# Packed diagonal attention blocks, transposed feature maps and fixed copy engines in a two-layer attention kernel

## The chip, the cores and the metric

One core of a Trainium2 chip runs the whole program. The time is device microseconds of one execution; the median of three runs of the kernel before is 514.66 us (514.08 to 518.85). The engines are named as in the profile: PE (TensorE matmul), PEld (its weight load), DVE (VectorE), ACT (ScalarE), POOL (GpSimd), SP (SyncE, which issues most transfers).

## What is computed

Two pairs of layers, A then B, each with a residual, on x of 1 x 2048 x 512 in bf16, 32 heads of 16 features:

```python
def _A_ref(x, wq, wk, wv, wo, beta):          # 4 segments of 512 tokens
    ...
    phi = lambda t: jnp.where(t > 0, t + 1.0, jnp.exp(t))
    for s in range(N):
        ...
        p = _softmax(logits + causal mask inside the segment)   # logits = q k^T / 4
        a_dot = p @ vs
        a_mem = (phi(qs) @ M) / (phi(qs) @ z + 1e-06)
        o = g * a_mem + (1.0 - g) * a_dot
        M, z = M + phi(ks)^T vs, z + sum(phi(ks))
    return o @ wo
def _B_ref(x, wqkv, w_phi, wo):               # linear attention over all tokens
    pq, pk = q @ w_phi, k @ w_phi
    phi_q = concat(softmax(pq), softmax(-pq)); phi_k likewise
    return ((phi_q @ (phi_k^T v)) / (phi_q @ sum(phi_k) + 1e-06)) @ wo
x = x + A(layernorm(x)); x = x + B(layernorm(x)); and both once more
```

## The kernel before

All of x stays in SBUF (`X`, 16 tiles of 128 tokens). A segment is four tiles. Scores are computed with the keys on the partitions, so that one exponential yields the weights of the product with the values, and a 17th column of the values gives the softmax's sum.

**Attention of a segment** (`a_att`, L1152) runs over pairs of query tiles, (0,1) and (2,3); in the last segment over (0,1), (2) and (3), `LAST` at L1392. Head features are 16 wide; keys are kept twice, with the odd or the even heads set to zero (`KT`, `KTo`), so that 32 rows of PE serve one head. A strip is one PSUM pair of banks of 128 x 1024: matmuls of 32 rows, two or one query tiles wide. Each strip gets one exponential on ACT (L1199) into a `PT` buffer (12 of them, L850), and its diagonal blocks are masked by POOL with `affine_select` (L1203). Two strips on different row groups are issued side by side (`rows`, `mate`). After the strips of a group of eight heads come the products with the values (17 columns each), a reciprocal (L1222) and a scaling for each tile (L1224), then the addition of the memory part `AM` (L1233), a transpose, the output projection and the residual (`a_out` L1243, `residual` L1239).

**Projections** (`a_proj`, L1057): at the first segment of each layer (`by_pe`) keys are projected feature-major for the scores (16 matmuls of 128 columns a tile) and once more token-major (4 matmuls of 512 columns, L1085) for phi (L1025: an exponential on ACT, a minimum and a maximum-plus-sum on DVE), which the memory state needs (`a_state`, L1108).

**Layer B**: `b_keys` (L1251) projects keys and values of a segment, takes both exponentials on ACT (L1261), sums and reciprocals on DVE (L1262, L1264), scales on POOL (L1266; DVE for the last two tiles), and adds into `KV32`; after the last segment `Rkv` (L1295) is formed. `b_queries` (L1300) makes the query features (`EQ`), `b_out` (L1337) the output. B's output of layer 0 runs beside A of layer 1; the last one is the tail, which stores the result.

**Order.** The kernel is written as a list of operations with reads, writes and a cost. `schedule` (L352) lays them on the engines in one pass of a list scheduler: of the operations that could start, the one with the least number in `PLAN` (L44, one number for each operation, in the order in which they are written down) goes first. An operation with two possible engines (`copy`, L784: ACT or DVE) takes the one where it can start earlier. `finalize` (L609) turns the dependencies into semaphore waits, so on the chip the order on each engine is fixed and the times are not. Where PE would be idle too long, idle matmuls are put in (L1448) to keep its clock up.

Of the kernel before, what the change touches and what calls it, by code (L numbers as in the profile page):

```python
# [15 lines left out]
H = 32  # L16
DH = 16
# [9 lines left out]
ENGS = ("pe", "act", "dve", "pool", "sp")  # L27
HOP = dict(pe=0.03, act=0.03, dve=0.03, pool=0.05, sp=0.04)
# [11 lines left out]
OVERLAP = 0.14  # L40
PRI = dict(mem=-5.0, state=0.5, aout=-0.2, lnx0=-0.5, lnx1=-10.0, ap0=9.5, aps=4.625, bo0=-6.0, bo1=3.5, lnb=-7.5, bk=2.0, bks=2.2, kv=14.0, q00=58.0,
# [3 lines left out]
    3, 4, 5, 7, 6, 0, 64, 10, 8, 9, 11, 14, 79, 15, 18, 13, 23, 29, 75, 32, 53, 21, 80, 26, 150, 35, 58, 85, 16, 126, 36, 156, 71, 60, 61, 122, 44,  # L45
    42, 285, 292, 20, 141, 151, 140, 194, 106, 100, 117, 57, 22, 12, 87, 81, 40, 2, 49, 17, 84, 82, 120, 47, 31, 48, 43, 1, 131, 113, 174, 19, 91,
    123, 52, 25, 59, 83, 41, 199, 28, 219, 65, 189, 191, 27, 62, 70, 45, 108, 97, 93, 39, 143, 181, 206, 88, 107, 105, 116, 56, 132, 133, 112, 24,
    154, 142, 127, 95, 157, 54, 37, 76, 186, 144, 51, 172, 188, 200, 134, 148, 192, 165, 135, 236, 218, 177, 149, 74, 248, 257, 266, 158, 69, 169,
    175, 287, 256, 114, 249, 291, 195, 119, 211, 164, 153, 136, 130, 99, 288, 180, 171, 230, 293, 261, 204, 265, 124, 197, 33, 63, 89, 182, 78, 50,
    159, 170, 227, 255, 121, 128, 138, 215, 110, 226, 213, 46, 187, 240, 98, 216, 55, 282, 260, 250, 273, 72, 320, 299, 269, 160, 176, 90, 198, 178,  # L50
    173, 212, 220, 238, 279, 244, 297, 329, 243, 317, 179, 335, 332, 252, 167, 246, 309, 294, 290, 286, 270, 348, 308, 306, 229, 253, 234, 366, 333,
    237, 67, 307, 389, 455, 399, 356, 233, 319, 208, 259, 328, 232, 231, 221, 271, 314, 339, 315, 362, 429, 318, 276, 324, 254, 380, 251, 205, 313,
    344, 360, 417, 454, 377, 342, 338, 353, 334, 387, 347, 382, 402, 416, 446, 376, 331, 401, 323, 361, 495, 396, 383, 235, 438, 436, 365, 464, 394,
    463, 349, 431, 459, 469, 392, 168, 435, 407, 444, 472, 450, 404, 476, 458, 405, 483, 453, 466, 451, 245, 397, 403, 447, 517, 635, 521, 530, 500,
    509, 406, 364, 263, 262, 300, 374, 224, 375, 486, 359, 482, 534, 478, 499, 582, 528, 491, 492, 529, 434, 553, 595, 511, 669, 525, 583, 596, 572,
    533, 38, 66, 145, 102, 155, 161, 77, 147, 185, 30, 125, 96, 103, 163, 111, 109, 92, 73, 321, 311, 296, 203, 386, 330, 340, 423, 357, 388, 275,
    351, 400, 202, 410, 384, 258, 484, 452, 391, 352, 363, 395, 385, 368, 418, 432, 201, 370, 425, 424, 341, 515, 422, 398, 354, 409, 420, 503, 477,
    414, 516, 488, 591, 543, 536, 547, 379, 373, 326, 346, 371, 481, 277, 412, 310, 440, 419, 426, 514, 618, 301, 558, 441, 494, 498, 538, 549, 546,
    465, 487, 457, 433, 523, 214, 34, 68, 101, 184, 118, 217, 129, 86, 193, 302, 268, 225, 152, 312, 139, 350, 267, 280, 274, 281, 272, 305, 284, 322,
    415, 146, 358, 283, 372, 408, 166, 456, 367, 442, 627, 639, 674, 449, 550, 545, 518, 602, 575, 666, 462, 390, 461, 437, 421, 210, 540, 467, 413,  # L60
    460, 470, 445, 617, 493, 513, 471, 604, 489, 519, 508, 662, 657, 631, 510, 640, 764, 625, 660, 679, 655, 690, 664, 701, 724, 837, 758, 846, 673,
    696, 719, 769, 795, 771, 838, 733, 824, 1351, 1380, 1496, 1373, 1318, 1407, 1302, 1304, 1126, 1231, 1201, 1209, 1505, 1467, 1360, 1563, 1434,
    1500, 1595, 1462, 1424, 1567, 1532, 1576, 1425, 1757, 1733, 1596, 1646, 615, 672, 532, 654, 697, 652, 680, 698, 714, 703, 678, 427, 570, 577, 650,
    734, 369, 381, 295, 552, 496, 574, 555, 621, 597, 554, 475, 548, 448, 663, 541, 506, 593, 522, 505, 520, 524, 468, 637, 560, 563, 677, 624, 638,
    587, 692, 526, 649, 694, 798, 581, 571, 504, 544, 535, 598, 556, 630, 613, 497, 539, 629, 573, 584, 607, 603, 623, 659, 706, 502, 501, 485, 578,
    592, 566, 542, 537, 608, 559, 616, 576, 611, 619, 562, 646, 695, 626, 738, 737, 818, 754, 588, 620, 601, 606, 605, 653, 568, 658, 569, 599, 645,
    636, 622, 633, 614, 585, 586, 490, 667, 740, 751, 676, 642, 807, 704, 793, 800, 836, 687, 675, 716, 799, 634, 651, 641, 632, 561, 691, 686, 565,
    689, 699, 700, 710, 661, 763, 743, 708, 439, 813, 829, 759, 746, 723, 791, 775, 861, 713, 839, 756, 712, 776, 762, 773, 788, 770, 801, 772, 711,
    786, 720, 768, 564, 811, 750, 778, 779, 855, 888, 806, 808, 822, 827, 814, 732, 685, 753, 845, 820, 939, 889, 804, 789, 902, 830, 643, 828, 883,
    872, 908, 869, 927, 886, 958, 875, 862, 856, 914, 916, 957, 895, 945, 936, 241, 183, 190, 264, 228, 239, 343, 336, 327, 411, 137, 196, 104, 162,  # L70
    209, 94, 303, 304, 337, 430, 600, 612, 551, 567, 527, 647, 671, 531, 590, 925, 966, 926, 1007, 985, 730, 823, 802, 670, 644, 721, 693, 656, 681,
    628, 665, 705, 843, 702, 707, 783, 728, 832, 792, 648, 731, 715, 742, 755, 739, 774, 825, 682, 870, 803, 741, 780, 819, 726, 579, 849, 787, 557,
    428, 507, 810, 752, 580, 748, 844, 831, 729, 782, 897, 834, 900, 747, 725, 867, 871, 479, 594, 345, 727, 684, 709, 760, 745, 805, 683, 797, 833,
    781, 668, 766, 877, 1064, 962, 784, 717, 1018, 1000, 688, 809, 876, 812, 874, 899, 898, 906, 777, 722, 857, 840, 835, 826, 790, 969, 912, 920,
    842, 858, 903, 994, 901, 963, 1066, 954, 1129, 1096, 1014, 1009, 1164, 1021, 1005, 761, 1161, 1057, 1025, 1039, 1030, 1035, 1040, 1109, 940, 1136,
    989, 1144, 1045, 1029, 817, 1031, 1042, 937, 1026, 1043, 1061, 1083, 1151, 1008, 1038, 1046, 1015, 1149, 896, 1134, 1121, 1063, 1036, 1127, 1217,
    1269, 1493, 1510, 1084, 1171, 1170, 1143, 1049, 1206, 996, 1053, 1123, 1069, 1059, 1140, 1065, 1106, 1067, 841, 735, 854, 880, 971, 1041, 1101,
    1011, 1003, 961, 864, 1060, 955, 1047, 1062, 981, 1087, 1050, 1102, 952, 1022, 1110, 1157, 1128, 1056, 1158, 1006, 1048, 1027, 953, 976, 959,
    1079, 1113, 1028, 1054, 1111, 998, 1017, 1037, 1119, 951, 1090, 1154, 1001, 1104, 1077, 1051, 1116, 1071, 1118, 1159, 1112, 1058, 1117, 1240,
    1241, 1088, 1080, 1160, 1108, 982, 1130, 1082, 997, 1098, 1172, 1074, 1162, 1076, 1175, 1153, 1147, 1232, 1230, 1024, 1182, 1242, 1250, 1207,  # L80
    1270, 885, 821, 848, 744, 892, 894, 922, 923, 873, 610, 609, 907, 933, 918, 850, 749, 868, 863, 757, 950, 924, 932, 860, 930, 1010, 796, 765, 851,
    893, 960, 816, 917, 991, 852, 965, 905, 949, 935, 904, 964, 934, 944, 815, 891, 974, 878, 980, 986, 1002, 859, 1055, 947, 1033, 1004, 968, 847,
    853, 909, 1019, 1034, 972, 882, 992, 1013, 785, 794, 983, 987, 984, 973, 943, 967, 1044, 1023, 1091, 1032, 1142, 1103, 956, 884, 866, 938, 1068,
    1125, 1244, 1204, 1132, 1146, 1156, 1163, 1150, 1233, 1152, 1180, 1073, 1093, 1433, 1094, 1358, 1099, 1178, 1252, 1095, 1374, 1200, 1181, 1251,
    1189, 1248, 1139, 1328, 1215, 325, 393, 298, 316, 278, 355, 474, 443, 589, 473, 242, 115, 223, 289, 222, 247, 512, 480, 378, 207, 921, 929, 910,
    887, 736, 970, 928, 915, 879, 913, 919, 1190, 993, 1020, 718, 865, 881, 911, 942, 890, 946, 1078, 1115, 1089, 1052, 1107, 1085, 990, 767, 948,
    999, 978, 1092, 988, 1097, 979, 1105, 1070, 1075, 1184, 1208, 1277, 1016, 977, 975, 1174, 1081, 1120, 1218, 1249, 1166, 1265, 1273, 1196, 1221,
    1247, 1100, 941, 931, 995, 1234, 1188, 1316, 1122, 1303, 1352, 1193, 1253, 1263, 1375, 1131, 1306, 1259, 1239, 1195, 1312, 1495, 1411, 1410, 1283,
# [91 lines left out]
    3424, 3397, 3445, 3300, 3431, 3443, 3417, 3451, 3435, 3407, 3404, 3439, 3442, 3378, 3296, 3295, 3420, 3398, 3415, 3369, 3367, 3448, 3426, 3441,  # L180
    3352, 3358,
)


class Res:

# [1309 lines left out]
```

## Time and profile before

| | |
|---|---|
| median of three runs | 514.66 us |
| the profiled execution | 518.92 us |
| its span, first to last instruction | 517.3 us |
| PE clock granted, mean | 0.987 |
| idle matmuls (L1450) | 125, 19.7 us |
| exponentials of scores (L1199) | 320, all between 17.5 and 463.7 us |
| products with the values (17 columns) | 2560 |
| row statistics (L1007), DVE | 64 of 683 ns |
| residuals (L1241), DVE | 54 of 682 ns |
| sums of key features (L1262), DVE | 32 of 1212 ns |
| key feature exponentials (L1261), ACT | 64 of 611 ns |

A busy time is the union of an engine's instructions; the mean of a group is of one instruction, from start to modelled end, so that pipelined matmuls add up to more than their busy time. In the last line of each group stands the idle time of the engine just before it and what ended it.

### The profile page before, as it was taken

The numbers are of one execution on the slowest core, as the hardware profiler recorded it, in microseconds if no ns is written. First come the engines' busy times: TensorE is split into PE (matmuls) and PEld (weight loads), VectorE is DVE, ScalarE is ACT, GpSimd is POOL, SyncE is SP. The second block draws the span as 40 slices with busy tenths as digits, with TensorE's granted clock in tenths as the row PEclk, the third lists the DMA queues.
The fourth block names the chain that finished last, engine by engine and source line by source line (L and its number), as shares of the span: only waits on it lengthen the run. The fifth ranks groups of instructions, "written<-read, shape, count | busy, mean of one in ns | idle before, by whom it ended". The sixth has DMA issues, their size and how long they took to land.

```text
span 517.3 us, 16946 instructions
## 1 busy us (share of the span) xinstructions
PE 487.7 (94%) x7194; PEld 306.4 (59%) x7286; DVE 432.3 (84%) x1025; ACT 440.3 (85%) x593; POOL 269.8 (52%) x396
## 2 busy tenths in 40 slices
PE   9989999999999999999999999999999999999997
PEld 6656455656456656656665555655555555565664
DVE  6998789968669888899968788988998677887995
ACT  3989999989999999854599999899999999974443
POOL 5464486635567766230147468456854476631234
PEclk9989999989999999999999999999999999997999
DMA  8956433332200411200115425224433121110034
GB/s 240 272 93 94 79 67 53 38 57 46 49 13 15 59 39 22 26 4 5 22 22 74 55 39 94 54 41 64 63 63 63 23 55 33 13 37 4 4 82 142
DMA packets 94538, 29.96 MB, mean 58 GB/s; under 512 B 86272, under 2 KB 94464, under 8 KB 94464
## 3 DMA queue, kind: packets, MB, share of 16 engines
q1 hardware_dynamic: 93216, 27.83, 30.0%
q10 hardware_dynamic: 1248, 1.06, 0.8%
q8 instruction: 57, 0.93, 0.8%
q14 instruction: 17, 0.14, 0.1%
HBM read 6.32 MB, written 2.10 MB: 16 GB/s over the span
## 4 chain that ended last, share of the span: by engine, by line
PE 52%; ACT 32%; DVE 11%; DMA 2%; issue 2%
PE PS L729 48%; ACT PT L1199 25%; PE PS L1450 3%; DMA xnT<-xn 2%; ACT Ek L1261 2%; ACT phi L1027 2%; DVE stats L1007 1%; PE PS L807 1%; DVE X L1241 1%; DVE O L1358 1%; DVE KV L1293 1%; DVE EQ L1332 1%; DVE Rkv L1295 1%; DVE rd L1357 0%; DVE PhiK L1029 0%
## 5 line engine op out<-in xcount | busy, mean ns | idle before, releaser
L1199 ACT ACTIVATE PT<-PS 128x1024 bf16<-128x1024 f32 x320 | 308.2, 1054 | 10.0 <-PE PS L729 9.1
L1203 POOL TENSOR_SCALAR_AFFINE_SELECT PT<-PT 128x512 bf16<-128x512 bf16 (+2 forms) x280 | 169.7, 617 | 131.7 <-ACT PT L1199 128.0
L729 PEld LDWEIGHTS PS<-VT,PT 128*128 128x128 bf16 x2560 | 78.1, 96 | 23.3 <-issue 5.8
L729 PE MATMUL PS<-VT,PT 128*128 128x17 bf16 x2560 | 85.7, 171 | 0.1
L729 PE MATMUL PS<-QT,KT 32*128 32x256 bf16 (+1 forms) x864 | 77.4, 245 | 4.5 <-ACT PT L1199 2.9
L1266 POOL TENSOR_TENSOR Ek<-Ek,rZ 128x1024 bf16<-128x1024 bf16 x28 | 55.3, 1977 | 44.7 <-DVE rZ L1264 44.7
L729 PE MATMUL PS<-QT,KTo 32*128 32x128 bf16 (+1 forms) x864 | 76.1, 243 | 2.4 <-ACT PT L1199 1.0
L729 PEld LDWEIGHTS PS<-QT,KT 32*128 32x128 bf16 x864 | 32.4, 92 | 39.2 <-ACT PT L1199 24.0
L1261 ACT ACTIVATE Ek<-PS 128x512 bf16<-128x512 f32 x64 | 35.8, 611 | 13.1 <-PE PS L729 12.8
L729 PEld LDWEIGHTS PS<-QT,KTo 32*128 32x128 bf16 x864 | 35.0, 93 | 19.6 <-ACT PT L1199 11.6
L1241 DVE TENSOR_TENSOR X<-X,PS 128x512 bf16<-128x512 bf16 x54 | 36.8, 682 | 11.3 <-PE PS L729 10.7
L1262 DVE TENSOR_REDUCE Zk<-Ek 128x64 f32<-128x1024 bf16 x32 | 38.6, 1212 | 8.2 <-ACT Ek L1261 7.9
L1007 DVE BATCH_NORM_STATS2 stats<-X 128x6 f32<-128x512 bf16 x64 | 43.3, 683 | 1.5 <-DMA X<-in_A_x_dram 0.8
L1013 POOL TENSOR_TENSOR rstd<-rstd,negh 128x2 f32<-128x2 f32 (+1 forms) x38 | 26.3, 694 | 33.3 <-DVE rstd L1011 32.1
L729 PE MATMUL PS<-xnT,WA_q 128*128 128x128 bf16 x512 | 35.9, 221 | 0.1
L729 PE MATMUL PS<-WA_v,xnT 128*128 128x512 bf16 x110 | 31.9, 380 | 2.4 <-issue 1.0
L729 PE MATMUL PS<-WA_k,xnT 128*128 128x512 bf16 x111 | 31.4, 380 | 2.8 <-issue 1.0
L729 PEld LDWEIGHTS PS<-xnT,WA_q 128*128 128x128 bf16 x512 | 29.6, 99 | 7.0 <-issue 2.8
L1224 DVE TENSOR_TENSOR O<-PS,r 128x128 bf16<-128x128 f32 x128 | 31.5, 281 | 1.2
L729 PE MATMUL PS<-WA_o,OT 128*128 128x512 bf16 x115 | 30.0, 380 | 1.4 <-issue 0.6
L729 PE MATMUL PS<-WB_o,OT 128*128 128x512 bf16 x118 | 29.6, 380 | 1.4 <-DVE QT L785 0.5
L1017 DVE TENSOR_SCALAR xn<-X,mv,rstd 128x512 bf16<-128x512 bf16 x64 | 26.9, 430 | 2.0 <-DMA xnT<-xn 0.9
(135 smaller groups left out, 839.1 us busy)
## 6 DMA issues: line engine op xcount, KB each, us to landing
out_dram<-X SPq DMA_DIRECT2D x16, 128.0 KB, 1.8
X<-in_A_x_dram SPq DMA_DIRECT2D x3, 512.0 KB, 10.0
EQ<-in_B_wqkv_dram SPq DMA_DIRECT2D x2, 512.0 KB, 10.5
OT<-O SPq DMA_TRANSPOSE x46, 2.5
xnT<-xn SPq DMA_TRANSPOSE x36, 2.5
WA_o<-in_A_wo_dram SPq DMA_DIRECT2D x1, 512.0 KB, 10.1
WB_v<-in_B_wqkv_dram SPq DMA_DIRECT2D x1, 512.0 KB, 12.3
WB_o<-in_B_wo_dram SPq DMA_DIRECT2D x1, 512.0 KB, 9.9
```

The lines of the kernel that those rows point to most:

```text
L729: return e.matmul(o, l, r, start=st, stop=sp, tile_position=(basep(l), basep(o)))
L1007: self.dve(lambda e, t=t: e.bn_stats(self.stats[:, t, :], self.X[:, t, :]), 0.60, [R("X", t)], [R("stats", t)])
L1013: self.pool(lambda e, ve=ve, n=n: e.tensor_tensor(ve, ve, self.negh[:, 0:1].to_broadcast([128, n]), ALU.pow), 0.76, [R("rstd", t0 + i) for ...
L1017: self.dve(lambda e, t=t, xn=xn: e.tensor_scalar(xn.ap[:], self.X[:, t, :], self.mv[:, t, 0:1], self.rstd[:, t:t + 1], op0=ALU.subtract, o ...
L1199: self.act(lambda e, st=st, pt=pt: e.activation(pt.ap[:].rearrange("p b c -> p (b c)"), self.ps[:, st.slot[0] * 512:st.slot[0] * 512 + 102 ...
L1203: self.pool(lambda e, dv=dv, nd=nd: e.affine_select(dv(), dv(), [[0, 2], [0, nd], [1, 128]] if nd > 1 else [[0, 2], [1, 128]], ALU.is_ge, 0.0,
L1224: self.dve(lambda e, r1=r1, view=view, c=c, g=g: e.tensor_tensor(o[c].ap[:, g, :].rearrange("p (h d) -> p h d", d=DH), view()[:, c, :, 0:1 ...
L1241: self.dve(lambda e: e.tensor_tensor(X[:, t, :], X[:, t, :], self.bank(gen), ALU.add), 0.61, [R("X", t), gen()], [R("X", t)])
L1261: self.act(lambda e, sgn=sgn, Ek=Ek, gen=gen: e.activation(Ek.ap[:, sgn, :], self.bank(gen), ACT.Exp, scale=1.0 - 2.0 * sgn), 512, [gen()] ...
L1262: self.dve(lambda e, Ek=Ek, Zk=Zk: e.tensor_reduce(Zk.ap[:], Ek.ap[:].rearrange("p s (h j) -> p s h j", h=H), AX.X, ALU.add), 1.15, [Ek(0) ...
L1266: scale = lambda e, Ek=Ek, rZ=rZ: e.tensor_tensor(Ek.ap[:].rearrange("p s (h j) -> p (s h) j", j=DH), Ek.ap[:].rearrange("p s (h j) -> p ( ...
L1450: ins = e.matmul(self.ps[:, b * 512:b * 512 + 256], self.warm[:, 0:128], self.warm[:], start=True, stop=True)
```

## The change

1. **Diagonal blocks packed.** In the odd tiles of each pair the two halves of 64 tokens are exchanged in `X` (loads and stores are split accordingly). The scores of the first halves of both tiles' diagonals, for all four groups of heads, go into one extra pair of strips (`ta`, one for each `y`): matmuls of 32 rows, 64 keys and 64 queries, first tile on partitions 0 to 63 and second on 64 to 127. The rest of the two diagonal tiles goes into one strip per group and `y`, whose exponential writes the middle of a wider buffer (`DT`, 4 buffers of 2 x 2 x 384). POOL masks three blocks of 64 queries, one of them copied from `ta`; DVE makes the fourth as the minimum of `ta` and a constant `late`, which is 0 or 3e38. `PT` has 7 buffers, `O` has 2, and `O2` holds both tiles of a pair. The last segment runs in pairs too.
2. **Per pair**: one reciprocal and one scaling for both tiles, one addition of `AM` of 128 x 1024.
3. **Phi of the first keys**: where keys are projected feature-major and phi is wanted, it is taken from that projection and transposed by DMA; the token-major projection falls away there.
4. **Residual by PE**: in the last segment's `a_out`, and in B's output of the first chunk at the layer change, X is added by a matmul with the identity, followed by a copy on ACT or DVE.
5. **Engines**: `ON` lists 63 operations for ACT, 74 for DVE and 3 (`Rkv`) for POOL; `PLAN` is a new list of 3539 numbers (3455 before). Key scaling on POOL is two halves of 128 x 512.
6. Smaller: `vtone` set by one copy per buffer; the helpers `PAIR`, `second` and `xa` are there and switched off.

```diff
+PAIR = 0.0
...
+        for e, some in ON.items():
+            for i in some:
+                ops[i].eng = (e,)
...
-        self.p_PT = slots("PT", 12, [128, 2, 512], BF16)
+        self.p_PT = slots("PT", 7, [128, 2, 512], BF16)
+        self.p_DT = slots("DT", 4, [128, 2, 2, 384], BF16)
...
+            flat = s <= 2 and tt in by_pe
+            if flat:
+                fm = lambda a: a[:].rearrange("p (g c) -> p g c", g=NG)
+                self.phi(t2, lambda t2=t2: fm(t2.ap), lambda gen=gen: self.bank(gen).rearrange("p (g c) -> p g c", g=NG), gen, t2(), shape=fm)
+                self.transposed(lambda tt=tt: seg["PhiK"].ap[:, tt, :].rearrange("p (a c) -> p a c", a=4), lambda t2=t2: t2.ap[:], [t2()], [seg["PhiK"](tt)], False, pre=[seg["PhiK"]])
...
+        i0, i1 = ts
+        full = [[(0, j), (1, j)] for j in range(i0)]
...
+        ta = [self.p_PT.tile() for _ in range(2)]
+        for y in range(2):
+            st = strips(y, ta[y], lambda st, y=y: [x for g in range(NG) for par in range(2) for h in range(2) for b in range(2) for x in [
+                mm(st, b, (2 * g + par) * 64, K2[par], 2 * y + b, g, ts[h] * 128 + 64 * h, 64, 192 * h, 64, p=64 * h)]], kr)
...
+            for y in range(2):
+                dt = self.p_DT.tile()
+                st = strips(y, dt, lambda st, y=y, g=g: [x for par in range(2) for b in range(2) for x in [
+                    mm(st, b, par * 256, K2[par], 2 * y + b, g, i0 * 128, 128, 64, 192)]] + [x for par in range(2) for b in range(2) for x in [
+                    mm(st, b, par * 256 + 192, K2[par], 2 * y + b, g, i1 * 128, 128, 128, 64)]], kr)
...
+                select(0, 0, src=early)
+                P.add(("dve",), lambda e, early=early, block=block: e.tensor_tensor(block(320), early(), self.late[:, None, None, :].to_broadcast([128, 2, 2, 64]), ALU.min),
+                      {"dve": 0.2}, [ta[y](), R("late")], [dt(("x", 320))], lat=0.09, port=True)
+                select(64, 64)
+                select(256, 0, 64)
...
+            mms.append((lambda: (self.bank(gen), self.ident[:], self.X[:, t, :], False, True), 512))
...
-        PAIRS, LAST = ((0, 1), (2, 3)), ((0, 1), (2,), (3,))
+        PAIRS, LAST = ((0, 1), (2, 3)), (((0, 1), (2, 3)))
```

## The prediction

> **What bounds the kernel now.** I read the page's busy times first, then five windows cut at the first and last exponential (L1199) of each layer: start, attention of layer 0, switch, attention of layer 1, tail.
>
> ```profile
> PE 487.7 (94%) x7194; PEld 306.4 (59%) x7286; DVE 432.3 (84%) x1025; ACT 440.3 (85%) x593; POOL 269.8 (52%) x396
> ```
> ```profile
> 0.00:17.50 17.50, 16.21 (x149) 12.01 (x152) 12.53 (x50) 7.49 (x13) 7.12 (x19) 1.00 0.89 269
> 17.50:215.70 198.20, 186.22 (x3008) 116.32 (x3046) 165.92 (x384) 190.66 (x244) 119.74 (x179) 0.98 0.37 58
> 215.70:262.70 47.00, 45.51 (x531) 30.26 (x535) 42.52 (x98) 26.10 (x49) 6.68 (x7) 1.00 0.06 12
> 262.70:463.70 201.00, 191.69 (x3070) 117.86 (x3107) 169.24 (x401) 192.98 (x249) 120.81 (x179) 1.00 0.31 50
> 463.70:517.30 53.60, 48.09 (x447) 29.95 (x452) 42.06 (x94) 23.04 (x43) 15.50 (x12) 0.94 0.21 57
> ```
>
> Columns: length, then busy time of PE, PEld, DVE, ACT, POOL. In the two attention windows (399.2 us) ACT is busy 383.6 us (96%), DVE 335.2 (84%), POOL 240.6 (60%). PE's 95% there overstates it, as the waits and the timeline show:
>
> ```profile
> PEld PS L729 <- ACT PT L1199: 39.4, 101, 1.1
> ...
> ACT PT L1199 <- PE PS L729: 9.1, 19, 1.1
> ```
> ```profile
> 209.50 0.75 PE L729 MATMUL PS<-VT,PT 128*128 128x17 bf16 x24
> ...
> 267.05 0.23 PE L729 MATMUL PS<-QT,KT 32*128 32x128 bf16 x4
> 267.11 0.22 PE L729 MATMUL PS<-QT,KTo 32*128 32x128 bf16 x4
> 267.17 0.28 PE L729 MATMUL PS<-QT,KT 32*128 32x256 bf16 x4
> ```
>
> PE waits for exponentials 39.4 us, the exponentials for PE only 9.1. A 17-column matmul is booked 171 ns (its group's mean), yet 24 of them take 0.75 us, 31 ns each. So ACT bounds attention. Switch and tail run at half of ACT's pace: DVE is busy 90% of the switch, and the chain of waits runs there through DVE and then PE's projections.
>
> **Packed diagonals, ACT.** Today a segment has 40 exponentials of 128x1024, a quarter of each diagonal block (early queries, late keys) being wholly masked. Now the early-half corners of both tiles share one strip: pair (0,1) takes 2+4x2=10, pair (2,3) 2+4x6=26. 36 x 8 segments = 288, not 320. The output of the diagonal ones is strided; no row shows that, the 1006 to 1220 ns spread of L1199 bounds it, and I keep its mean:
>
> ```profile
> L1199 ACT ACTIVATE PT<-PS 128x1024 bf16<-128x1024 f32 x320 | 308.2, 1054 | 10.0 <-PE PS L729 9.1
> ...
> L1203 POOL TENSOR_SCALAR_AFFINE_SELECT PT<-PT 128x256 bf16<-128x256 bf16 x80 | 33.1, 419 | 10.1 <-ACT PT L1199 7.8
> ...
> L1233 DVE TENSOR_TENSOR O<-O,AM 128x512 bf16<-128x512 bf16 x24 | 12.3, 524 | 0.2
> ```
>
> 32 x 1.054 = 33.7 us less on ACT, all in attention: 349.9 left.
>
> **DVE.** Added: 128 minima with the constant `late`, 128x256. Nearest is L1233, 524 ns at twice the size, 0.27 by proportion; ends 0.20 (its least is 373, halved) and 0.52 (no gain from the smaller size). 128 x 0.27 = 34.6 (26 to 67). Removed: 128 products of 281 ns become 64 of twice the size; with 0.68 us at four times the size (L1358) the line through both gives 0.41, so 36.0-26.5 = 9.5. Reciprocals 72 to 64: about 1. The 24 additions of 524 ns become 12 of about 0.75: 3.6. Attention's DVE: 335.2+34.6-14.1 = 355.7 us.
>
> A rule weighs against this. The Trainium skill, "SBUF — State Buffer", section Who interferes with whom, says that a DVE instruction with two SBUF inputs and a GpSimd instruction reading SBUF exclude each other for a whole instruction. Were every minimum to wait out one 0.419 us select, DVE would have 53.6 us more. The trace agrees in kind (L1233 goes from 373 to 1470 ns, median 424), but its mean already holds such waits. None of the other numbers uses this sentence.
>
> **POOL.** 280 selects (110.4+33.1+28.2 = 171.7 us busy) become 8 segments x 2 pairs x 4 groups x 2 x 3 = 384 at 0.41 = 157. Ek's 28 products of 1.98 us become 56 halves; each pays the fixed part again (about 0.2), 5 us. POOL stays near 58%: nothing. But two selects (0.8 us) follow each diagonal exponential, and the product with values waits for them and the minimum. Behind it on PE stand the next strips, and ACT behind those. Cover: exponentials of the next group, while a PT buffer is free (second rival).
>
> **PE.** 32 strips less, 16 pairs of some 0.25 us: -4. New strips: 64 matmuls of 64 columns per pair of strips. Four 128-column ones start every 60 ns (15 ns each), the 17-column ones every 31; so 64 cost 0.5 (half of 15 ns) to 2.0 us. I take 1.0, the score row being nearest: 16 us. Eight plus four residuals go in by an identity matmul at about 0.22: +2.6. Keys' second projection at each layer's start falls: 32 matmuls at 0.215 = -6.9. Net about +8, covered by PE's 39.4 us of waiting for ACT.
>
> The rule against it: the Trainium skill, "TensorEngine Tiling (Array Packing)", sections Instruction Overhead and Gotcha 2, gives each matmul some 60 cycles however short and denies column tiles the fast weight load. By it the new strips sit at the upper end. No run here shows column tiles. It only weighs on the third rival's chance.
>
> **Plan and copies.** 140 operations get a fixed engine (63 ACT, 74 DVE, 3 POOL). Attention's ACT and DVE together hold 349.9+355.7 = 705.6 us, 353 each if the plan levels them. Today's joint share is 718.8/399.2 = 180 of 200%. With that share 392 us; with ACT's 96% on both, 367. DVE reaches 90% in the switch beside a busy PE, so I take both at 92.5%: 381, -18 us.
>
> **Start** (17.5 us): of the removed projection some 11 matmuls lie before the first exponential, 2.4 us on PE; loads hide part (DMA share 0.89): -1.5, ends 0 and -2.4. The odd tiles' half loads add two issues near 0.5 us on SP's queue ahead of weights: +0.5 (0 to 1). Four phi transposes of about 1.27 us each join SP's full queue (weights' transposes, 19.6 to 30 us); the tiles they delay are used first at 62 us (Ek), so nothing; without that cover 5 us.
>
> **Switch** (47 us): PE chain 242 to 262.7: -3.45 (16 matmuls) +0.9 = -2.6. DVE: six residuals of 0.68 become copies that ACT (26 of 47 us busy) can take, -4.1. But tiles 2 and 3 of segment 3 now end together: statistics, rows, key sums, reciprocal and scaling of tile 2 (0.68+0.17+0.43+1.21+0.54+1.20 = 4.2) move behind the last exponential. Its key exponentials started 5.7 us before tile 3's (223.5 and 229.2), so +2 (0 to 4). Net -0.6. The 4 phi transposes meet an idle queue (DMA share 0.06).
>
> **Tail**: the same delay, +2, less one Rkv product on POOL beside DVE: +1.5. Store halves: 8 more issues, the last one +0.5.
>
> Edits that move nothing: the row normalisation is already DVE's alone (L1017, all 64); the set-up of `late` (3 small POOL operations) and 8 copies merged to 2; `PAIR` is 0, so the new rules of the scheduler stay off; the tail's POOL list names the same tiles.
>
> **Sum**: -18 -1 -0.6 +2 = -17.6 us of the profiled 517.3 us span (518.92 us execution). The median of three is 514.66, so 514.66 x (1-17.6/517.3) = 497.
>
> **Rivals.**
> 1. *ACT alone counted* (DVE fits beside it). 349.9/0.96 = 364, -35, in all -35: 480. For: DVE's waits are mostly on PE and ACT. Against: DVE would have to run at 98%. 12%.
> 2. *PT buffers stop ACT; slower.* PT falls from 12 to 7, two held all pair long by the shared corners; five serve groups needing four. With 36 exponentials in some 48 us, a group of six lasts 8 us; a buffer may be held 5x8/4 = 10 us. I count strip and queue 1.5, rest of its group 4 to 6, selects 0.8 to 1.2, values 56x31 ns = 1.7: 8 to 10.4. Past 10, each us more costs ACT 0.8 a group, in 32 groups 26 us. From 0.7 us beyond, the 18 us are gone; at 1.3 beyond, +33, in all +16: 530. For: no spare at the upper end. Against: diagonal strips can be put first, so that selects lie under the other four. 12%.
> 3. *DVE or PE becomes the bound.* Strips of 2 us on PE (+16) use up its waits and the joint share stays 180%: 392, in all -7. Or minima take 0.52: 32 us more on DVE, at 92.5% (705.6+32)/1.85 = 399, in all 0. So 508 to 515. For: DVE gets the added work and no spare engine takes minima. Against: both prices are ends. 18%.
> 4. *The change does not do what it says*: strips saved but the plan's copies pile on one engine, ACT still 96% at 370: 385, as the forecast; no number of its own, within its chance.
>
> **Chances.** Forecast 58% (own range 487 to 507), rivals 12, 12, 18. One per cent is 5.1 us, about what a measurement of this kernel can tell from no change: 509.5 to 519.8. Faster: 58+12+8 (the part of the third below 509.5) = 78%; within: 10%; slower: 12%, the second rival. Range 480 to 514: it leaves out the second rival and half of the first.
>
> **What would show it.** Right: L1199's successors 288 times, near 1.05 us; ACT in attention 350 to 365 us, DVE 345 to 360, attention windows near 190 us each; switch near 46. Wrong: ACT idle before exponentials for PE strips that wait for values or selects (buffers); minima well over 0.3 us; attention windows near 200 us with DVE over 95%; the corner strips near 2 us on PE.

## The result and the profile after

| | before | after |
|---|---|---|
| median of the runs taken with it | 515.82 us (514.08 to 518.85) | 538.32 us (533.05 to 538.51) |
| ratio | | 1.0405, 95% interval 1.0322 to 1.0488 |
| the profiled execution, its span | 518.92, 517.3 us | 538.30, 536.6 us |
| granted clock, mean of the span | 0.987 | 0.941 |
| clock loss, (1 - clock) x span, mean of runs | 3.9 us | 26.8 us |

The kernel became some 21 us slower by the ratio, 22.5 by the medians, where 18 us faster was forecast. Medians below are over all runs of a kernel; the ratios leave out runs that lay over 1.5% above its fastest. The busy times of the page of after:

```profile
PE 516.5 (96%) x8165; PEld 333.5 (62%) x8165; DVE 444.0 (83%) x1038; ACT 424.3 (79%) x581; POOL 265.4 (49%) x532
```

ACT lost 16 us; DVE gained 12 and PE 29. Of PE's 29 us, 8 are idle matmuls: 192 of 28.0 us where before had 125 of 19.7, with 51 more in the longer start and 24 more in the tail. The five windows of after, cut at its own exponentials as those of before were (columns: length, then PE, PEld, DVE, ACT, POOL, clock, DMA share, GB/s):

```profile
0.00:23.40 23.40, 21.41 (x222) 17.37 (x223) 14.02 (x46) 7.53 (x13) 7.63 (x22) 1.00 0.99 232
23.40:224.70 201.30, 193.90 (x3405) 124.94 (x3405) 167.44 (x390) 180.92 (x237) 116.76 (x242) 0.92 0.37 57
224.70:265.40 40.70, 40.65 (x477) 26.03 (x477) 37.80 (x84) 24.99 (x47) 7.99 (x10) 1.00 0.05 10
265.40:477.50 212.10, 208.12 (x3525) 131.35 (x3525) 178.40 (x425) 184.25 (x240) 116.23 (x242) 0.93 0.31 50
477.50:536.60 59.10, 52.38 (x552) 33.77 (x552) 46.33 (x96) 26.59 (x50) 16.74 (x17) 0.99 0.24 54
```

Against before, the start is 5.9 us longer, attention 3.1 and 11.1, the tail 5.5; only the switch is shorter, by 6.3. In attention PE is busy 97% at a clock of 0.92 to 0.93, ACT 88%. The waits turned round: ACT's exponentials waited 9.1 us for PE before, and 32.6 (19.0 + 9.5, and 4.1 for those of the corners) now:

```profile
ACT DT L1307 <- PE PS L804: 19.0, 28, 2.0
...
PEld PS L804 <- ACT PT L1297: 12.8, 33, 0.8
...
ACT PT L1297 <- PE PS L804: 9.5, 14, 1.8
...
PEld PS L804 <- ACT DT L1307: 8.3, 20, 0.8
```

The costliest groups of the page, for what was added:

```profile
L1313 POOL TENSOR_SCALAR_AFFINE_SELECT DT<-DT 64x256 bf16<-64x256 bf16 (+1 forms) x256 | 107.6, 439 | 88.6 <-ACT DT L1307 87.8
L1307 ACT ACTIVATE DT<-PS 128x1024 bf16<-128x1024 f32 x128 | 130.9, 1040 | 19.5 <-PE PS L804 19.0
L1297 ACT ACTIVATE PT<-PS 128x1024 bf16<-128x1024 f32 x128 | 128.3, 1039 | 10.5 <-PE PS L804 9.5
...
L1313 POOL TENSOR_SCALAR_AFFINE_SELECT DT<-PT 128x256 bf16<-128x256 bf16 x128 | 56.5, 448 | 65.4 <-PE PS L804 47.8
...
L1317 DVE TENSOR_TENSOR DT<-PT,late 128x256 bf16<-128x256 bf16 x128 | 43.9, 351 | 4.5 <-PE PS L804 3.9
```

With the 32 of the corners (L1286, 1031 ns) the exponentials are the 288 forecast, and the strided ones (L1307) cost what the others do. Nothing here is dear enough for 20 us. The granted clock in 40 slices is what stands out, first before, then after:

```profile
PEclk9989999989999999999999999999999999997999
```
```profile
PEclk9965989999999999999999999999999956799999
```

Half clock was granted at 29.8 to 53.7, 429.2 to 449.6 and 453.1 to 463.3 us and in two short spells, 61 us in all; before, 13.6 us. And one place in PE's timeline of after, where a corner strip (tiles 32*64) is issued side by side with a strip of 128-wide tiles:

```profile
426.52 0.22 PE L804 MATMUL PS<-QT,KT 32*64 32x64 bf16 x4
...
426.73 0.53 PE L804 MATMUL PS<-QT,KT 32*64 32x64 bf16 x6
427.19 0.40 PE L804 MATMUL PS<-QT,KTo 32*128 32x192 bf16 x4
427.52 0.20 PE L804 MATMUL PS<-QT,KT 32*128 32x64 bf16 x2
427.65 0.35 PE L804 MATMUL PS<-QT,KTo 32*64 32x64 bf16 x4
```

Four corner matmuls start every 31 to 50 ns until 426.73; from there on the two strips alternate by twos, and the last 16 matmuls take about 1.2 us (the view merges neighbours, so its counts mix the two strips). At full clock such a pair lasts 1.41 us until the next work starts, a corner strip by itself 0.38, a strip of 8 by itself 0.33. There are 13 such pairs: 10 with a strip of 8, 3 with a strip of 4 (0.94 us).

### The profile page after: what moved, and what is told of

Its sections match the earlier page's. It is cut to its first block, busy times and chain, and to the rows that moved or that the text cites. A ratio compares the mean times of both kernels' runs of the same rounds, so it can differ in the third digit from the quotient of the medians.

```text
span 536.6 us, 18995 instructions
## 1 busy us (share of the span) xinstructions
PE 516.5 (96%) x8165; PEld 333.5 (62%) x8165; DVE 444.0 (83%) x1038; ACT 424.3 (79%) x581; POOL 265.4 (49%) x532
## 4 chain that ended last, share of the span: by engine, by line
PE 64%; DVE 13%; ACT 13%; DMA 5%; SPq 3%; issue 1%; POOL 1%
PE PS L804 62%; ACT DT L1307 4%; ACT PT L1297 4%; SPq L868 3%; DMA X<-in_A_x_dram 2%; DMA EQ<-xn 2%; DVE DT L1317 1%; PE PS L1585 1%; ACT PT L1286 1%; DMA OT<-O 1%; DVE VT L860 1%; PE PS L882 1%; ACT Ek L1388 1%; ACT EQ L1440 1%; DVE AM L1255 1%
## 5 line engine op out<-in xcount | busy, mean ns | idle before, releaser
L1313 POOL TENSOR_SCALAR_AFFINE_SELECT DT<-DT 64x256 bf16<-64x256 bf16 (+1 forms) x256 | 107.6, 439 | 88.6 <-ACT DT L1307 87.8
L1307 ACT ACTIVATE DT<-PS 128x1024 bf16<-128x1024 f32 x128 | 130.9, 1040 | 19.5 <-PE PS L804 19.0
L1297 ACT ACTIVATE PT<-PS 128x1024 bf16<-128x1024 f32 x128 | 128.3, 1039 | 10.5 <-PE PS L804 9.5
L804 PE MATMUL PS<-QT,KT 32*64 32x64 bf16 (+3 forms) x1280 | 86.1, 231 | 4.3 <-ACT PT L1297 1.4
L1313 POOL TENSOR_SCALAR_AFFINE_SELECT DT<-PT 128x256 bf16<-128x256 bf16 x128 | 56.5, 448 | 65.4 <-PE PS L804 47.8
L804 PE MATMUL PS<-VT,DT 128*128 128x17 bf16 x1536 | 80.0, 171 | 0.6 <-DVE X L1360 0.2
L804 PE MATMUL PS<-QT,KTo 32*64 32x64 bf16 (+3 forms) x1280 | 78.9, 226 | 0.0
L804 PEld LDWEIGHTS PS<-VT,DT 128*128 128x128 bf16 x1536 | 72.4, 97 | 10.3 <-issue 2.7
L1399 POOL TENSOR_TENSOR Ek<-Ek,rZ 128x512 bf16<-128x512 bf16 x56 | 58.7, 1065 | 29.8 <-DVE rZ L1391 26.7
L804 PEld LDWEIGHTS PS<-QT,KTo 32*128 32x128 bf16 (+1 forms) x1280 | 44.5, 103 | 2.5
L1286 ACT ACTIVATE PT<-PS 128x1024 bf16<-128x1024 f32 x32 | 32.6, 1031 | 4.1 <-PE PS L804 4.1
```

The costliest lines, as they stand in the source:

```text
L804: return e.matmul(o, l, r, start=st, stop=sp, tile_position=(basep(l), basep(o)))
L1286: self.act(lambda e, st=st, pt=ta[y]: e.activation(pt.ap[:].rearrange("p b c -> p (b c)"), self.ps[:, st.slot[0] * 512:st.slot[0] * 512 + ...
L1297: self.act(lambda e, st=st, pt=pt: e.activation(pt.ap[:].rearrange("p b c -> p (b c)"), self.ps[:, st.slot[0] * 512:st.slot[0] * 512 + 102 ...
L1307: self.act(lambda e, st=st, dt=dt: e.activation(dt.ap[:, :, :, 64:320], self.ps[:, st.slot[0] * 512:st.slot[0] * 512 + 1024].rearrange("p ...
L1313: lambda e, c=c, src=src, base=base, p=p, block=block: e.affine_select(block(c, p), src() if src else block(c, p), [[0, 2], [0, 2], [1, 64 ...
L1399: self.pool(lambda e, Ek=Ek, rZ=rZ, sgn=sgn: e.tensor_tensor(Ek.ap[:, sgn, :].rearrange("p (h j) -> p h j", j=DH), Ek.ap[:, sgn, :].rearra ...
```

## The experiments

Three theories stood at first: the *clock theory* (half clock takes the time), the *work theory* (PE has more to do, the mixed pairs above all) and the *buffer theory* (the prediction's second rival). Line numbers in a run's views are those of that run's own kernel.

**e1_rows: DVE's queue at the start.** The first statistics of segments 1 and 2 are put behind the copy of the values that PE waits for.

```diff
+        q = P.queues["dve"]
+        held = [786, 796, 364, 366, 367]
...
+        q[at:at] = held
```

> The changed kernel with one order altered on DVE: the row statistics of layer 0's segments 1 and 2 (four, with one aggregation), which stood idle until rows of x had landed, go behind the copy of VT that PE waits for at 28.2 us. Clock theory (the time is lost while PE is granted half its clock, 61 us after against 14 before, and the first long stretch is set off by this wait): PE stays busy, the stretch from 29.8 to 53.7 us goes or shrinks to one window of 3.4 us, and the time falls by 8 to 14 us to 525-530. Work theory (packed strips make PE's work longer, the clock follows from nothing else): within 3 us of the changed kernel, 535-540. Buffer theory (7 PT buffers stop ACT): no change.

539.32 us, ratio 1.0401 (1.0289 to 1.0514): nothing. DVE's copy came 4 us earlier, but PE's gap of 3 us at 28 us stayed, now in the middle of one operation's 16 matmuls and put down to "issue", so the clock dropped as in after. One transfer of the instruction queue (28.4 to 29.5 us) falls into that gap; that PE waited for it is not shown. The edit did not remove the gap, and tells nothing of the clock theory.

**e2_warm, e3_rows_warm: the clock held up.** Idle matmuls before score strips where PE streams little; e3 also has the edit of e1.

```diff
+EXTRA = {300: 1, 304: 1, 586: 2, 590: 1, 614: 2, 608: 1, 644: 6, ...}
...
+                    if e == "pe" and op.i in EXTRA:
+                        b = [t for t in op.tiles if getattr(t, "kind", None) == "st"][0].slot[0]
+                        self.idle[0](eng, EXTRA[op.i], b)
```

> The changed kernel with 57 idle matmuls of 256 columns (6.2 us of PE) placed ahead of 28 score strips, in the stretches after 35 us in which fewer than 43% of a 3.4 us window were streamed. Clock theory: the stretches at half clock from 429 to 463 us go, the first one stays; the time falls by 6 to 14 us, 524-532. Work theory: PE is the bound and has 6 us more to do, so 540-545. Buffer theory: no change.

> Both alterations together. Clock theory: granted clock near 0.98 as before, the time 510-520, that is the changed kernel less its 24 us of surplus lost clock, plus a few. Work theory: 540-545. Buffer theory: 536-540.

534.29 (ratio 1.0315, 1.0247 to 1.0383) and 531.21 (1.0277, 1.0212 to 1.0343). The mean clock loss fell from 26.8 to 18.1 and 15.9 us, the time by 4.0 and 7.1 us although 6.2 us of PE work was added: the clock has a share. How large, these two can't say, since the idle work was added with it.

**e4_apart: the mixed pairs issued one after the other.**

```diff
+        for op in P.ops:
+            if op.mate is not None and len(op.mms) != len(op.mate.mms) and 32 in (len(op.mms), len(op.mate.mms)):
+                op.mate = None
```

> The changed kernel, where a corner strip of 32 matmuls is issued side by side with a strip of 4 or 8 (13 pairs, 0.94 to 1.41 us each against 0.38 for a corner strip alone and 0.33 for a strip of 8): these 13 pairs are issued one after the other. Work theory: some 13 x 0.6 = 8 us less on PE, and 5 to 10 us less time, 528-533. Clock theory: no direct change; within 4 us, unless a long stretch at half clock goes by chance, which the granted clock would show. Buffer theory: no change.

523.89 us, ratio 1.0113 (1.0042 to 1.0185): 14.4 us less than after, more than the 5 to 10 expected. Three of the four runs lie at 521.9 to 525.8 us, the fourth at 533.2; by the means of after and of these three it is 13.8. By the pairs' own durations 10 x (1.41 - 0.71) + 3 x (0.94 - 0.70) = 7.7 us were to be had. The clock loss of the three fell from 26.8 to 19.3 us; that the rest comes from it is an inference.

**e13_by_fours: what in the pair costs.** The pairs stay, alternating by fours; by this rule the three with a strip of 4 come out one after the other.

```diff
+                    by = 4 if len(op.mms) != len(beside.mms) and 32 in (len(op.mms), len(beside.mms)) else 2
+                    for k in range(0, lag + len(beside.mms), by):
```

> The changed kernel, in which the 13 side-by-side pairs of a corner strip (32 matmuls of 64 columns) with a strip of 4 or 8 alternate four matmuls at a time instead of two; nothing else. In the trace of after such a pair with a strip of 8 takes 1.41 us against 0.38 + 0.33 issued apart, while pairs of a strip of 8 with one of 4, of one tile width, take 0.34: length alone costs nothing. Alternation theory (each change between 64-wide and 128-wide tiles is paid, 7 of them a pair): 3 changes instead of 7, so a pair falls to some 1.0 us, and the time by a third to a half of e4_apart's gain: 525 to 533 us. Rival (two tile widths that are under way on the array at once cost, in whatever order): a pair stays at 1.3 to 1.4 us, 533 to 539.

527.47 us, ratio 1.0203 (1.0166 to 1.0239). The pair that stood at 426.52 in after, in PE's timeline of e13:

```profile
420.88 0.22 PE L805 MATMUL PS<-QT,KT 32*64 32x64 bf16 x4
...
421.09 0.39 PE L805 MATMUL PS<-QT,KT 32*64 32x64 bf16 x6
421.32 0.40 PE L805 MATMUL PS<-QT,KTo 32*128 32x192 bf16 x6
...
421.81 0.21 PE L805 MATMUL PS<-VT,PT 128*128 128x17 bf16 x2
```

From 420.88 to the next work at 421.81 it takes 0.93 us, not 1.41. Four changes of tile width fewer save 0.48 us, 0.12 us a change: the alternation theory holds. Issued apart, with one change, the same two strips take 0.70 us in e4, again 0.12 us for each of two changes. Unequal length is not the cause: the 12 pairs of 8 and 4 matmuls of one width that run through without a wait take 0.34 us in after, as long as 8 alone. Of the 10.9 us by which the median fell, 10 x 0.48 + 3 x 0.24 = 5.5 are the pairs' own.

**e5_apart_loads, e12_start: the late start.** Both reorder SP's loads as before's. e5 stands on e4's edit; e12 has the weights of phi in front, cuts early idle matmuls, and stands on e6.

```diff
+        want = [7, 1, 2, 4, 5, 11, 9, 13, 14, 15, 16, 18, ...]        # e5; e12: [17, 7, 1, 2, 4, ...]
+        at = [n for n, i in enumerate(q) if i in want]
...
+            for _ in range(1 if 3 < self.calls <= 7 else n):           # e12
```

> The changed kernel with its 13 uneven side-by-side strip pairs issued one after the other (as in e4_apart) and, besides, the loads on SP's queue put into the order of before (weights for keys, halves of tile 1 and 3, weights for queries, second half of the value weights, X rows of segment 1, then the rest). Load theory (the late start, first exponential at 22 to 23.4 us instead of 17.5, comes from the value weights and X rows standing behind loads that are used later): first exponential back to 17.5 to 19 us, row statistics no longer waiting about 2 us for X, no half-clock spell near 30 us; 4 to 6 us less than e4_apart, 518 to 520. Rival (the start is late because the work ahead of the first exponential was itself put in another order on PE, ACT and DVE; loads only follow): first exponential within 1 us of e4_apart's 22.0, time within 2 us of 523.9.

> e6_apart_warm with the weights of phi first on SP's queue and the other loads behind them in the order of before (e5_apart_loads had put the weights of phi late, and DVE stood 29 us for them), and with the idle matmuls of 10 to 18 us cut to one in each of four places. Load theory (the first exponential comes 5 to 6 us later than before because the X rows of tile 1 come late, and idle matmuls fill PE meanwhile): first exponential at 18 to 19.5 instead of 23.7 us, time 4 to 5 us below e6_apart_warm's 521.7: 516 to 518. Rival (what follows the first exponential, other projections and copies, is what takes the time): first exponential earlier, but layer 0's attention ends within 2 us of e6_apart_warm's 217, and the time is within 2 us of 521.7.

548.08 (ratio 1.0623, 1.0549 to 1.0697) and 535.50 us (1.0359, 1.0298 to 1.0420): two misses. In e5 DVE stood 28.9 us for the weights of phi, which its new queue needs early. In e12 the first exponential came at 21.8 us, 1.9 earlier than in e6 but no earlier than in e4 (22.0), which has none of these edits; and then DVE's queue stood before the statistics of segment 1, whose rows were now late, with the copy of the values behind them at 36.96 us (DVE's timeline of e12):

```profile
34.28 2.47 DVE L1103 BATCH_NORM_STATS2 stats<-X 128x6 f32<-128x512 bf16 x4 [10.70 <-DMA X<-in_A_x_dram]
```

The plan's load order and its engine queues belong together; the load theory's 4 to 5 us were not found, and why the start is 6 us late stays open.

**e6_apart_warm: unpaired and warm.** The edits of e4 and of e2, with 98 idle matmuls placed anew.

> The changed kernel with its 13 uneven pairs issued one after the other, and 98 idle 256-column matmuls (10.5 us of streaming at full clock) put in front of 45 score strips, in the stretches where e4_apart streamed less than 0.38 of a 3.4 us window. Clock theory: the half-clock spells that e4_apart still had (162-172, 418-435, 442-452 us, 37 us in all, at half the rate worth up to 18 us) mostly vanish, granted clock of the span 0.98 or more, and the time falls by 6 to 12 us net of the idle work, to 512 to 518. Work theory (PE is full in those stretches, its slow clock costs little beside the work): clock up, time within 3 us of e4_apart's 523.9, or longer by part of the 10.5 us.

521.70 us, ratio 1.0112 (1.0058 to 1.0167). Clock loss 5.1 us, near before's 3.9, but the time is only 2.2 us less than e4's median, and 0.3 less than that of e4's three lower runs, for 10.5 us of idle work added. By its own expectation this is the work theory's number. It doesn't show that the clock is free: idle work that takes what the clock gives would look the same. This is the best version of the changed kernel, and still about 5 us behind before. Its five windows:

```profile
0.00:23.70 23.70, 20.48 (x222) 16.82 (x223) 13.99 (x46) 7.62 (x13) 7.64 (x22) 1.00 0.97 229
23.70:218.20 194.50, 186.62 (x3442) 120.49 (x3443) 167.42 (x389) 180.51 (x237) 116.94 (x242) 0.98 0.38 59
218.20:259.00 40.80, 40.76 (x484) 26.15 (x484) 37.86 (x85) 25.09 (x47) 7.99 (x10) 1.00 0.05 10
259.00:464.30 205.30, 201.70 (x3577) 129.08 (x3574) 179.38 (x425) 183.98 (x240) 117.30 (x242) 0.98 0.31 52
464.30:522.60 58.30, 52.73 (x552) 33.63 (x552) 46.19 (x96) 26.60 (x50) 16.76 (x17) 1.00 0.22 54
```

Against before: start +6.2, attention -3.7 and +4.3, switch -6.2, tail +4.7. With 19 us less ACT work in it, and with the added idle matmuls, attention gained nothing: 399.8 us against 399.2.

**e7 to e11: what bounds before.** The premise itself, on the kernel before: ACT more, PE more, ACT less, PE less, both less. In e10 and e11 all exponentials also take the scale 0.0001 in place of 0.25.

```diff
+                    for a, z in (((0, 512), (512, 1024)) if self.count % 3 == 0 else ((0, 1024),)):    # e7
...
+        for op in [op for op in P.ops if op.rows][::3]:    # e8
+            op.mms[:] = [(f[0], f[1]) for f in op.mms[:4]] + op.mms
...
+                    w = 512 if self.count > 24 and self.count % 4 == 0 else 1024    # e9, e11
...
+        for op in [op for op in P.ops if op.rows and op.mate is None and op.i not in mates][24::2]:    # e10, e11
+            del op.mms[len(op.mms) // 2:]
```

> The kernel before, with every third 128x1024 exponential split into two of 128x512 (107 of 320). A 128x512 activation takes 0.60 us in its rows, so a split adds 2 x 0.60 - 1.05 = 0.15 us to ACT: 16 us in all, nothing else changed. If ACT bounds attention, as the prediction took it, all of it is seen: 531 to 534 us, ratio 1.03. If PE or the levelled plan bounds it as much, half or less: 518 to 525, ratio below 1.015. If attention were bound elsewhere: no change.

> The kernel before, with the first four matmuls of every third score strip issued twice (the same result into the same place). Four such matmuls take 0.11 (beside another strip) to 0.21 us (alone): 107 strips, 12 to 23 us added to PE, nothing else. The prediction took PE to have 39.4 us of waiting for exponentials as cover: then 0 to 3 us are seen, ratio below 1.006. If PE bounds attention as much as ACT does, most of it is seen: 527 to 538, ratio 1.02 to 1.045.

> The kernel before, in which every fourth 128x1024 exponential from the 25th on (74 of them) takes only its first 512 columns; the other weights are left at older values, and nothing else changes. In e7_before_act a split into two halves added 0.08 us of ACT time, so a half costs about 0.56 us and 74 x 0.48 = 36 us fall from ACT, as much as the 33.7 us that the prediction took off it. If ACT bounds attention (the prediction's premise), -18 to -35: 482 to 499 us. If PE bounds it about as much (e8_before_pe showed 5 of the 11 us added to PE, e7_before_act 1 to 4 of the 8 added to ACT), PE takes over at once: -3 to -12, 505 to 514. If PE alone bounds it: within 3 us of before.

> The kernel before, with the second half of the matmuls left out in every second score strip that is issued alone (83 strips, some 0.12 us each: 10 us off PE; those scores are older values, and all exponentials are taken at scale 0.0001 for that reason). ACT, DVE and POOL do what they did. If ACT bounds attention: within 2 us of before. If PE bounds it as much: -3 to -7 us, ratio 0.986 to 0.994, the mirror of e8_before_pe.

> The kernel before with both cuts, of e9_before_less_act and e10_before_less_pe. If the two engines bound attention in turns, the sum is more than the parts added: -15 to -25 us, 492 to 502. If ACT alone bounds it, the same time as e9_before_less_act; if PE alone, the same as e10_before_less_pe.

| | busy time moved, measured | ratio (95%) | us |
|---|---|---|---|
| e7 | ACT 440.3 to 445.9 | 1.0052 (1.0020 to 1.0084) | +2.7 |
| e8 | PE 493.8 (e7) to 504.7 | 1.0115 (1.0058 to 1.0172) | +5.9 |
| e9 | ACT 440.3 to 415.4 | 0.9891 (0.9849 to 0.9932) | -5.6 |
| e10 | some 10 us off PE, forecast | 1.0004 (0.9964 to 1.0044) | 0 |
| e11 | ACT to 413.9, PE to 474.9 | 0.9787 (0.9711 to 0.9863) | -11.0 |

The last column is (ratio - 1) x 516.8, the median of before with e9 to e11 (516.5 for e7, e8). PE of e8 is set against e7's, since before's trace lacks 92 matmuls. e9 cuts 25 us from ACT, and 5.6 are seen: ACT does not bound attention alone. What is next shows in e9's waits, where the exponentials wait for PE 25.4 us (before 9.1), as long as PE's weight loads wait for them:

```profile
PEld PS L729 <- ACT PT L1202: 27.7, 66, 1.0
ACT PT L1202 <- PE PS L729: 25.4, 45, 1.6
```

e10 alone gives nothing, which by its own expectation is what ACT as the bound would give. But e9 and e10 together give twice what e9 gives, though less than the 15 to 25 us expected, and of 10.9 us added to PE in e8 5.9 are seen: that speaks for two engines that bound attention in turns. Part of e10's missing gain may be the clock: with less to stream its mean clock loss rose from 3.9 to 7.7 us.

**e14_small_minima: DVE.** The minima of the corners on the base of e6, eight columns instead of 64.

```diff
+                    w = 64 if self.done <= 10 else 8
+                    return e.tensor_tensor(block(320)[:, :, :, 0:w], early()[:, :, :, 0:w], self.late[:, None, None, 0:w].to_broadcast([128, 2, 2, w]), ALU.min)
```

> e6_apart_warm with the minima of the corners, from the 11th on (118 of 128), made over 8 of 64 columns in each block (the other columns keep older values): about 0.25 of 0.35 us each, 30 us off DVE, nothing else. If DVE bounds attention in the changed kernel (the prediction's third rival; it is busy 84 to 87% there): 10 to 25 us less than e6_apart_warm, 497 to 512. If the minima lie beside PE's work: within 3 us of 521.7.

526.87 us, ratio 1.0177 (1.0081 to 1.0273), from runs of 522.7, 523.5, 530.3 and 535.3 us. Only 8 us left DVE (444.8 to 437.1), not 30: the median minimum fell from 285 to 175 ns, and one waited 3.95 us while POOL worked. Nothing of the 8 us is seen, and the interval is wide: no sign that DVE bounds, but at a quarter of the dose that was meant.

## Why the prediction was wrong

**What bounds the kernel: the step that failed.** I read "ACT bounds attention, PE waits 39.4 us for exponentials" out of the waits. Those 39.4 us are PEld's, and weight loads overlap PE; in the same windows PE itself was busy 186.2 and 191.7 of 399.2 us, idle 21. I set these 95% aside as overstated, because a 17-column matmul is booked 171 ns and starts every 31. But a busy time is a union and does not add overlapping bookings. e9 prices the error: a cut near the forecast's size, measured at 25 us, gave 5.6 us where the premise makes it nearly 25. So PE was a second bound and not 39.4 us of cover; e10, which gave nothing, is the one run of the five that doesn't fit this.

**ACT's term** of -33.7 us was right in count and in the mean of one, but neighbours overlap, so the exponentials' busy time fell by 29.0 us (308.2 to 279.2 for all 288 together). ACT's whole busy time fell by 16, since the new plan gave it 20 other operations (273 to 293); attention's ACT came to 365.2 us, not 349.9. Levelling ACT and DVE at 92.5% each left out PE, the third engine at its limit.

**Minima**: 351 ns on the mean against 270 taken: 45 us, not 34.6. The price was right for a minimum by itself (28 that met no POOL instruction average 273 ns); 100 that overlap one average 372. The longest of them, in DVE's and in POOL's timeline of after:

```profile
138.23 1.45 DVE L1317 TENSOR_TENSOR DT<-PT,late 128x256 bf16<-128x256 bf16 x1
```
```profile
138.06 0.41 POOL L1313 TENSOR_SCALAR_AFFINE_SELECT DT<-PT 128x256 bf16<-128x256 bf16 x1
138.45 1.05 POOL L1399 TENSOR_TENSOR Ek<-Ek,rZ 128x512 bf16<-128x512 bf16 x1
139.46 0.50 POOL L1313 TENSOR_SCALAR_AFFINE_SELECT DT<-DT 128x256 bf16<-128x256 bf16 x1
```

It stands through a select and a scaling and ends soon after them. The Trainium skill, "SBUF — State Buffer", section Who interferes with whom, has the two engines exclude each other; the trace agrees in kind, at about 10 us, 128 x (0.351 - 0.273), not the 53.6 of every minimum waiting out a select. That DVE bounds found no support in e14, which is too weak to exclude it. **Selects**: 384, as forecast, 164 us against 157.

**Corner strips on PE**: 0.38 us a strip, 0.76 a pair, against 1.0 forecast: right when alone. The Trainium skill, "TensorEngine Tiling (Array Packing)", section Instruction Overhead, gives each matmul some 60 cycles, which the prediction read as the upper end of 2.0; 32 in 0.38 us, 12 ns each, do not show that. What was missing is that 13 of them stand beside 128-wide strips: 7.7 us directly by durations, 14.4 us by e4, whose clock loss is also smaller. So "net +8, covered by PE's waiting" failed on both words.

**The clock was in no step and in no rival.** Over the runs of before, the fitted time rises about 1.0 us with each us of clock loss; over the four runs of after 0.5. The added loss of 22.9 us (26.8 - 3.9) is then worth some 11 to 23 us, an estimate from these fits; it overlaps with e4's 14.4 and isn't added to it. e4 and e6 together take 16.6 us off, three quarters of the 21.5 us between after and before (538.3 - 516.8). What is left, 4.9 us (5.3 in the profiled runs), is the balance of e6's windows, of which 10.5 us of idle matmuls are a part.

**Start** (-1 forecast, +5.9): wrong in sign; open after e5 and e12. In the other traces of the changed kernel with the plan's own load order the first exponential stands at 22.0 to 23.7 us, against 17.5. **Switch** (-0.6, -6.3): the residual by PE and the projection left out brought more than forecast; which of them was not tried. **Tail** (+1.5 and a store, +5.5): the mechanism is in the trace, work of tile 2 behind the last exponential. In e6's tail 64 products of values and key features stand where before had 32, and 8 matmuls of A's output projection where it had 4. The size was off, the more so because before's tail held a half-clock spell (464.2 to 471.0) that e6's has not.

**Rivals.** Buffers: PE's weight loads waited 1.7 us for selects in all; no. ACT alone: no. The third named PE as the bound, which e8 to e11 bear out in part, but priced it at 508 to 515 by dear strips. The rival on the slower side, the buffers, had the sign by luck: its cause was the wrong one.

## What to carry to other kernels

Before calling an engine the bound, read the idle time of the others' own busy line, not the waits of a queue that overlaps it; and where two engines stand at 95%, price a cut on one by what is free on the other. Matmuls that alternate between tile widths cost a change each: keep one width in a side-by-side pair. A schedule fixed in advance has also to be priced by what it does to the clock: a PE that is busy with short matmuls streams little.

## What the runs showed of the hardware

**Changes of tile width**: about 0.12 us for each change between 32*64 and 32*128 tiles (pairs of 1.41, 0.93 and 0.70 us with 7, 3 and 1 changes in after, e13 and e4); two strips of one width side by side pay nothing (0.34 us for 8 and 4 matmuls, 0.33 for 8 alone).

**The clock changes in steps of 3.4 us and does not come back at once.** All half-clock spells that end before the run does last 3.4 us or a multiple. With each matmul's columns counted at the rate of the 512-column ones (one every 0.215 us, all 128 rows), the windows of 3.4 us ahead of a drop in before and after streamed 0.13 to 0.44 of the time, most below 0.37; none above 0.45 was followed by one, but some 18 below it, the lowest at 0.34, were not either, so the share alone does not tell. At half clock, with the share taken of what that clock can stream, full clock returned after windows of 0.68 to 1.0 and stayed away after 0.51 to 0.81; in after, six windows of 0.54 to 0.81 followed each other from 30 to 50 us. These shares are estimates from the traces. The Trainium skill, "TensorE: Matmul & The Clock Gate", Part 1, has a window of 3.4 us and a drop after an idle one; the trace agrees on the length, but PE was not idle here: it was busy 98% of the attention of layer 1.

**Splitting is cheap on ACT**: an exponential split in two adds 0.08 us to ACT's busy time (316.3 - 308.2 over 106 splits), where I had taken 0.15. Neighbours overlap: the 214 whole and 212 half exponentials of e7 are booked some 369 us in all, within those 316.3.
